# Layer 2 of the first chunk reordered: batch 1's transposes ahead of the second sub-block, squares of v and pieces of sums moved

## The chip, the cores and the metric

The kernel runs on one core of a Trainium2 chip. The metric is the device time of one execution in microseconds (us), lower is better. A core has five engines that this document names as the profile does: PE (TensorE, matrix products; PEld is its loading of weights, which overlaps), DVE (VectorE), ACT (ScalarE), POOL (GpSimd) and SP (SyncE). Each engine executes its own instructions strictly in the order in which the program issues them, and waits at an instruction whose inputs, or whose output's space, are not ready. Transfers from and to main memory (DMA) are issued here from the queues of SP and POOL and run beside the engines.

## The reference

Attention over 8 batches of 8 heads, 576 positions and head dimension 64, followed by a two-layer network on the 4608 tokens:

```python
scores = scale * (q @ k.transpose(0, 1, 3, 2))          # 8 x 8 x 576 x 576
cum = np.cumsum(np.maximum(s, 0.0), axis=-1)
bias = -(cum[:, :, :, None] - cum[:, :, None, :])
scores = np.where(causal, -1e9, scores + np.minimum(bias, 0.0))
attn = softmax(scores)
x = (attn @ v).transpose(0, 2, 1, 3).reshape(4608, 512)
h = x @ w_in                                            # 512 -> 2048
g = 0.5 * h * (1.0 + erf(h / sqrt(2)))                  # exact gelu
out = g @ w_out                                         # 2048 -> 512
```

## The kernel before, in words

**Tiling.** The tokens are worked through in nine chunks of 512. A chunk needs the attention of a batch (576 tokens), so the loop `for c in range(NCH)` does, for chunk c, layer 1 and then layer 2, and puts the attention of batch c + 1 between the matrix products of layer 2. Nothing is scheduled by a planner: the order of the calls in the program is the order on each engine. PSUM, where PE writes, is given out by name: three slots `x`, `y`, `z` of two banks each and two single banks `M[0]`, `M[1]`. A slot is free again when the engine that reads the last result in it has done so.

**Attention of a batch.** `tr_one` (or `tr_two`) transposes q or k of four heads on PE (L395: 36 small products) and copies the result from PSUM to `qkT` (L402 if ACT copies, L404 if DVE does). `sc_mm(b, p, slots)` computes the scores of a pair of heads in two units (10 products, L434), each followed by one exp on ACT into `P` (L440). `mask` multiplies the diagonal blocks of `P` on DVE (L448 twice and L453 once for a pair). `scale_v` multiplies tiles of v by decay weights on DVE (L247, five tiles). `av_main` multiplies `P` with the weights and with v on PE (L463), after which `av_out` computes a reciprocal on ACT as ln and exp (L478, L479) for two halves of 256 columns and multiplies on DVE into `xT` (L503). `av_tails` does the last 64 positions at the start of the next layer 1. `av_main(b, 0)` reads pairs 0 and 2 of `P`, `av_main(b, 1)` pairs 1 and 3.

**Layer 1 of chunk 0** is `l1_item(c, f2)` for f2 = 0 to 7: eight products of 512 columns into slot `order[c][f2 % 3]` (L550) and a gelu on ACT (L558, the last one in two halves, L561). Item 7 writes the slot that item 4's gelu has read. The DVE computes `absmax` of four pairs meanwhile (L229).

**Layer 2 of chunk 0** is `l2_item(c, sub, f0, f1)` for four sub-blocks of 128 tokens (L576). Each sub-block sums over 16 products; they are issued as 8, 4 and 4, because the weights `w_out_r` arrive in four transfers of four rows each (POOL queue, L270). Sub-blocks 0 and 1 stand in `M[0]` and `M[1]`, 2 and 3 in the two halves of slot `y`. The last four products of a sub-block are followed by a copy to `o_sb` (on ACT for sub-blocks 0, 1, 2, on DVE for 3) and a store on SP's queue (L779). Since `order[1] = (y, z, x)`, the first item of chunk 1's layer 1 needs slot `y`, so it waits for the copy of sub-block 3.

Between these stand the transposes of batch 1's q and k (`tr_one(1, qd, i, eng, slot)`: qd 0 serves pairs 0 and 1, qd 1 pairs 2 and 3), its four `sc_mm`, masks, `scale_v(1, STS)` and the two `av_main`. Further there are

- `squares_v(b)`: the sum of squares of v on ACT (L237, two activations and two reads of the accumulator), used only by a check at the kernel's end;
- `exp_set()`: loads ACT's function table for exp and ln (L863); gelu needs another table (loaded before L558). Squares run with either table;
- `sums_b(which, f0, f1)`: differences of blocks of `w_out_r` into four tiles `Ts` on DVE (L743), for indices f0 to f1 of 8; index f needs rows 2f and 2f + 1 of `w_out_r`. Chunk 1's layer 2 is the first to read them. The fourth sum reads the second;
- `behind(1, w_out_r[0:1, FT - 5, 0:D])` and `load_v(1)`: a tiny transfer on SP's queue that waits for row 11 of `w_out_r`, so that the five transfers of batch 1's v (L225) start after it;
- `behind_v(1, 1)`: a tiny copy on POOL that waits for tile 1 of that v, followed in POOL's queue by four `load_front(2, ...)` (L106) and by `load_qk(3, "q")` (L197).

The loads of batch 1's q and k, `load_front(1, ...)`, are issued by POOL during the start of layer 1 (L106), among the loads of `w_out_r`.

Of the kernel before, what the change touches and what calls it, by code (L numbers as in the profile page):

```python
# [19 lines left out]
def kernel(  # L20
# [10 lines left out]
    nc = tc.nc  # L31
# [66 lines left out]
    def bank(slot, shape, dtype, name):  # L98

        return ps.tile(shape, dtype, tag=slot, bufs=1, name=name)  # L100
# [141 lines left out]
    def scale_v(b, sts, eng, h0=0, h1=H):  # L242
        t = raws[b, "v"]
        vb = vv[b % 2]
        for st0, st1 in sts:
            n_st = 128 if st1 < ST else SL
            eng.tensor_tensor(  # L247
                vb[:n_st, st0:st1, h0:h1, :],
                t[:n_st, st0:st1, h0:h1, :],
                wb[:n_st, st0:st1, b * H + h0 : b * H + h1]  # L250
                .unsqueeze(3).to_broadcast([n_st, st1 - st0, h1 - h0, D]),
                op=MULT,
            )

    STS = [(st, st + 1) for st in range(ST)]
# [150 lines left out]
    def tr_two(b, qd, i, engs):  # L406
        t_ps = [bank(m, [128, FR, 64], bf16, "tr_ps") for m in M]
        tr_mm(b, qd, i, t_ps)
        for pp in range(2):
            copy(  # L410
                engs[pp],
                qkT[b % 2][:, i, 2 * qd + pp, :S].rearrange("d (t r) -> d t r", r=FR),
                t_ps[pp].rearrange("d r t -> d t r"),
            )
# [485 lines left out]
    for c in range(NCH):  # L900
        nb = c + 1
        if nb >= B:
            l1_seven(c)
            if c < B:
                order[c + 1] = order[c]
            sums_a(c, (1, 2), HF // 2, HF)
            l2_seven(c)
            continue
        if c < 2:
            l1_item(c, 0, 0, KO - 2)  # L910
            l1_item(c, 1, 0, KO - 2)
            av_tails(c, M[0])
            l1_item(c, 0, KO - 2)
            l1_item(c, 1, KO - 2)
        else:
            l1_item(c, 0, 0, KO - 2)
            l1_item(c, 0, KO - 2)
            l1_item(c, 1)
        if 1 < c:
            transpose_tiles(nb)  # L920
            if nb + 1 < B:
                behind_g(qkT[nb % 2][0:1, 1, NP - 1, S - 1 : S])
                for n in "qk":
                    load_qk(nb + 1, n)
        for p in range(NP) if c == 0 else (0, 1) if c == 1 else (0, 1, 2):
            absmax(c, p)
        for f2 in range(2, FT // 2):
            l1_item(c, f2)
            if c == 1 and 2 <= f2 < 6:
                tr_two(2, f2 // 2 - 1, f2 % 2, both)  # L930
            if c == 1 and f2 == 2:
                squares_v(1)
                load_qk(3, "k")
            if c == 1 and 3 <= f2 < 5:
                scale_v(2, STS[f2 - 3 : f2 - 2], nc.vector)
            if c == 1 and f2 == 5:
                sums_a(c, (1, 2, 3), 0, HF // 2)
                scale_v(2, STS[2:4], nc.vector)
                squares_v(2)
            if c > 1 and f2 == 3:  # L940
                scale_v(nb, [(0, 4), (4, 5)], nc.vector)
                sums_a(c, (1, 2, 3), 0, HF // 2)
                absmax(c, 3)
                if c == B - 2:
                    sums_u((1, 2))
                    absmax(nb, 0)
            if c > 1 and f2 == 4:
                squares_v(nb)
                if nb + 1 < B:
                    behind(2, raws[nb + 1, "k"][0:1, ST - 2, 0, :])  # L950
                    load_v(nb + 1, [nc.sync])
        if c == 0:
            squares_v(0)
            sums_b((1, 2, 3, 4), 0, 4)
            exp_set()
            x, y, z = order[0]
            l2_item(c, 0, 0, 8)
            l2_item(c, 1, 0, 8)
            tr_one(1, 0, 0, nc.vector, z)
            tr_one(1, 0, 1, nc.scalar, x)  # L960
            l2_item(c, 2, 0, 8, y)
            sc_mm(1, 0, (z, x))
            l2_item(c, 3, 0, 8, y)
            sc_mm(1, 1, (z, x))
            mask(1, 0, nc.vector)
            sums_b((1, 2, 3), 4, 8)
            behind(1, w_out_r[0:1, FT - 5, 0:D])
            load_v(1, [nc.sync])
            l2_item(c, 0, 8, 12)
            l2_item(c, 1, 8, 12)  # L970
            tr_one(1, 1, 0, nc.vector, z)
            tr_one(1, 1, 1, nc.scalar, x)
            mask(1, 1, nc.vector)
            sums_b((4,), 4, 8)
            behind_v(1, 1)
            for qd in range(2):
                for n in "qk":
                    load_front(2, n, qd)
            l2_item(c, 2, 8, 12)
            l2_item(c, 3, 8, 12)  # L980
            sc_mm(1, 2, (z, x))
            l2_item(c, 0, 12, eng=nc.scalar)
            sc_mm(1, 3, (z, x))
            mask(1, 2, nc.vector)
            scale_v(1, STS, nc.vector)
            l2_item(c, 1, 12, eng=nc.scalar)
            l2_item(c, 2, 12, eng=nc.scalar)
            mask(1, 3, nc.vector)
            av_main(1, 0, M[0], z)
            l2_item(c, 3, 12)  # L990
            av_main(1, 1, M[1], x)
            order[1] = (y, z, x)
            load_v(2, [nc.sync])
            load_qk(3, "q")
        else:
            exp_set()
            sums_a(c, (1, 2), HF // 2, HF)

            x, y, z = order[c]
            order[nb] = (z, x, y)  # L1000
            add = nc.vector.tensor_tensor
            al_t = bank(M[0], [128, 2, 256], fp32, "o_al")
            al = [al_t[:, u] for u in range(2)]
            kept = [keep_sb(i, n) for i, n in enumerate(("q0", "k0", "q1"))]
            oa = [two_sb() for _ in range(2)]

            prod(c, 1, al, start=True)
            sc_mm(nb, 0, (z, x))
            sc_mm(nb, 2, (y,))
            copy(nc.vector, kept[0], al_t)  # L1010
            if c == 1:
                scale_v(2, STS[4:5], nc.vector)
                load_v(3, [nc.sync])
            be = bank(M[1], [128, 2, 256], fp32, "o_be")
            prod(c, 2, [be[:, u] for u in range(2)], start=True)
            prod(c, 6, al, 0, 6)
            mask(nb, 0, nc.vector)
            add(oa[0][:, :, N1], be, kept[0], op=ALU.add)
            sc_mm(nb, 2, (z,), 1)
            sc_mm(nb, 1, (x, y))  # L1020
            mask(nb, 2, nc.vector)
            prod(c, 6, al, 6)
            copy(nc.vector, kept[1], al_t)
            mask(nb, 1, nc.vector)
            sc_mm(nb, 3, (z, x))
            sums_a(c, (3, 4), HF // 2, HF)
            sums_a(c, (4,), 0, HF // 2)
            ga_t = bank(M[1], [128, 2, 256], fp32, "o_ga")
            ga = [ga_t[:, u] for u in range(2)]
            prod(c, 5, ga, start=True)  # L1030
            mask(nb, 3, nc.vector)
            if nb + 1 < B:
                behind_g(P_of[nb, 3][0:1, 1, PW - 1 : PW])
                cast_qk(nb + 1)
            den = bank(z, [128, 2, 512], fp32, "av_d")
            o = av_pe(nb, 0, den[:, 0], y)
            av_out(nb, 0, den[:, 0], o)
            prod(c, 7, al)
            copy(nc.scalar, kept[2], al_t)
            o = av_pe(nb, 1, den[:, 1], x)  # L1040
            add(oa[1][:, :, N2], ga_t, kept[2], op=ALU.add)
            av_out(nb, 1, den[:, 1], o)
            prod(c, 4, al)
            if c == B - 2:
                sums_x(c + 1, nc.vector)
            av_tails(nb, y)
            copy(nc.scalar, oa[1][:, :, N1], al_t)
            if c == B - 2:
                nc.scalar.preload_act_table_set("gelu_and_others")
            store(c, 2, oa[1])  # L1050
            prod(c, 3, ga)
            add(oa[0][:, :, N2], ga_t, kept[1], op=ALU.add)
            store(c, 1, oa[0])
            if c == 1:
                absmax(1, 2)
                absmax(1, 3)
                square(7)
            elif nb < B - 1:
                square(c + 1 if c > 2 else 0)
            if c == 2:  # L1060
                cert_decay()
            if c == B - 2:
                sums_u((3,))
# [4 lines left out]
    with tc.If(rv > 0):  # L1068
        with tc.tile_pool(name="gen", bufs=1) as gen, tc.tile_pool(
# [26 lines left out]
            with tc.For_i(0, B, 1) as b:  # L1096
# [8 lines left out]
                for h in range(H):  # L1105
# [17 lines left out]
                    for it in range(ST):  # L1123
# [9 lines left out]
                        x = gen.tile([128, S], fp32, tag="gx", bufs=2, name="gx")  # L1133
# [88 lines left out]
```

## Time and profile before

| | |
|---|---|
| median of 3 runs | 314.04 us (313.4 to 314.63) |
| the profiled execution, its own time | 314.03 us |
| its span, first to last instruction | 312.2 us |
| granted TensorE clock | 0.994 |
| layer 1 of chunk 0 on PE | 22.4 to 36.8 us of the span |
| layer 2 of chunk 0 on PE | 36.8 to 59.4 us |
| layer 1 of chunk 1 on PE | from 59.4 us |

The profile is one execution; times in it count from the first instruction. A row of the timeline reads: start, busy time, engine, line, operation, output, inputs, shape, count, and in brackets how long the engine had stood idle and what ended that. A row of a busy PE does not say that products run at full rate; the end of a product overlaps the start of the next, so a step's length is taken from one start to the next start. In the view of groups a row ends with busy time, mean ns of one, and the idle time before them. A row of transfers ends with the time from issue to landing.

### The profile page before, as it was taken

How to read it: one execution, taken by the hardware profiler on the slowest of the kernel's cores; microseconds unless marked ns; L12 is line 12 of the kernel's file. 1: busy time of each engine (PE TensorE's matmuls, PEld its weight loads, DVE VectorE, ACT ScalarE, POOL GpSimd, SP SyncE). 2: the span in 40 equal slices, each digit the busy share in tenths (PEclk: the TensorE clock that was granted, in tenths of full speed). 3: DMA queues.
4: the chain of work that ended last, by engine and by line, in shares of the span. 5: the costliest groups of instructions: out<-in, count | busy, mean ns of one | idle time of the engine just before them, and what ended most of it. 6: DMA issues, size and time to landing. Idle time of an engine off the chain costs nothing.

```text
span 312.2 us, 8460 instructions
## 1 busy us (share of the span) xinstructions
PE 293.0 (94%) x3522; PEld 194.8 (62%) x3522; DVE 228.4 (73%) x430; ACT 246.7 (79%) x348; POOL 98.8 (32%) x180
## 2 busy tenths in 40 slices
PE   0689999999999999999999999999999999999991
PEld 0564444545784578547854786477647887887780
DVE  3597337788879777696876597748798889856770
ACT  3687687798968996989788988798879877967830
POOL 6585007104070376228530944095500000000000
PEclk9999999999999999999999999999999999999997
DMA  7999999996616696969597859967891030011013
GB/s 110 200 180 206 206 166 188 270 237 155 132 24 193 120 221 127 256 116 214 116 277 140 186 121 232 208 156 150 171 249 20 2 135 5 0 69 68 2 47 98
DMA packets 77933, 45.07 MB, mean 144 GB/s; under 512 B 63168, under 2 KB 70336, under 8 KB 77888
## 3 DMA queue, kind: packets, MB, share of 16 engines
q1 hardware_dynamic: 67104, 24.93, 35.0%
q0 software_dynamic: 10784, 19.53, 32.1%
q8 instruction: 29, 0.48, 0.7%
q14 instruction: 16, 0.13, 0.2%
HBM read 36.85 MB, written 9.44 MB: 148 GB/s over the span
## 4 chain that ended last, share of the span: by engine, by line
PE 84%; DVE 5%; ACT 5%; DMA 2%; issue 1%; POOL 0%; ACTq 0%; POOLq 0%
PE h_ps L550 32%; PE o_al L764 17%; PE o_ga L764 9%; PE h_ps L667 6%; PE sc_ps L434 5%; PE o_be L764 4%; PE av_o L463 4%; PE av_d L463 2%; DMA fk<-in_k_dram 2%; PE o_ps L576 2%; ACT junk L237 2%; ACT P L440 2%; DVE vv L247 2%; PE av_t L463 1%; PE tr_ps L395 1%
## 5 line engine op out<-in xcount | busy, mean ns | idle before, releaser
L550 PE MATMUL h_ps<-xT,w_in_r 128*128 128x512 f16 x480 | 106.4, 379 | 0.5 <-DVE o_sb L404 0.5
L550 PEld LDWEIGHTS <-w_in_r 128*128 128x128 f16 x480 | 46.3, 98 | 53.9 <-issue 0.8
L440 ACT ACTIVATE P<-sc_ps 128x1024 bf16<-128x1024 f32 x64 | 60.2, 1032 | 3.4 <-PE sc_ps L434 3.3
L558 ACT ACTIVATE gT<-h_ps 128x1024 f16<-128x1024 f32 x49 | 48.3, 1018 | 13.2 <-PE h_ps L550 13.0
L764 PEld LDWEIGHTS <-S 128*128 128x128 f16 x512 | 47.8, 98 | 8.4 <-issue 0.9
L229 DVE TENSOR_REDUCE amx<-qkT 128x2 f32<-128x1152 bf16 x32 | 41.6, 1345 | 0.3 <-DMA qkT<-qk_bf 0.3
L764 PEld LDWEIGHTS <-gT 128*128 128x128 f16 x384 | 36.5, 98 | 7.6 <-issue 2.2
L448 DVE TENSOR_TENSOR P<-P,tri_bf 128x512 bf16<-128x512 bf16 x64 | 25.9, 420 | 11.3 <-ACT P L440 10.7
L754 DVE TENSOR_TENSOR S<-gT 128x1024 f16<-128x1024 f16 (+1 forms) x30 | 21.6, 722 | 14.0 <-ACT gT L561 12.1
L764 PE MATMUL o_al<-T,S 128*128 128x256 f16 x256 | 31.7, 273 | 0.0
L197 POOL DMA_DIRECT2D raw_k<-in_k_dram x25 | 21.1, 850 | 13.8 <-DMA raw_v<-in_v_dram 13.8
L434 PE MATMUL sc_ps<-qkT 64*128 64x256 bf16 (+2 forms) x320 | 22.3, 264 | 3.0 <-DVE qkT L404 1.7
L503 DVE TENSOR_TENSOR xT<-av_o,ln 128x256 f16<-128x256 f32 (+2 forms) x72 | 23.8, 387 | 1.6 <-ACT ln L479 1.2
L247 DVE TENSOR_TENSOR vv<-raw_v,wb 128x512 bf16<-128x512 f32 (+2 forms) x25 | 24.0, 1002 | 0.0
L197 POOL DMA_DIRECT2D raw_q<-in_q_dram x25 | 21.1, 858 | 0.9 <-POOL seen_v L148 0.9
L434 PEld LDWEIGHTS <-qkT 64*128 64x128 bf16 x320 | 13.9, 98 | 12.0 <-issue 6.7
L237 ACT ACTIVATE junk<-raw_v 128x2048 bf16<-128x2048 f32 (+1 forms) x16 | 20.3, 1268 | 0.3
L404 DVE COPY qkT<-tr_ps 128x576 bf16<-128x576 bf16 (+1 forms) x15 | 12.0, 834 | 10.1 <-PE tr_ps L395 10.1
L681 DVE TENSOR_TENSOR k<-h_ps,k 128x512 f32<-128x512 f32 (+1 forms) x12 | 11.3, 956 | 8.1 <-PE h_ps L667 5.5
L479 ACT ACTIVATE ln<-ln,lnb 128x256 f32<-128x256 f32 x32 | 16.3, 509 | 1.0
L148 POOL CAST seen_v<-qkT 1x1 f32<-1x1 bf16 x4 | 1.2, 304 | 48.5 <-DMA qkT<-qk_bf 48.5
L463 PE MATMUL av_o<-P,vv 128*32 128x256 bf16 (+1 forms) x512 | 16.5, 270 | 0.0
(132 smaller groups left out, 439.2 us busy)
## 6 DMA issues: line engine op xcount, KB each, us to landing
raw_v<-in_v_dram SPq DMA_DIRECT2D x32, 256.0 KB, 4.8
out_dram<-o_sb SPq DMA_DIRECT2D x14, 512.0 KB, 4.0
raw_q<-in_q_dram POOLq DMA_DIRECT2D x20, 256.0 KB, 4.6
raw_k<-in_k_dram POOLq DMA_DIRECT2D x20, 256.0 KB, 6.6
w_out_r<-in_moe_w_out_dram POOLq DMA_DIRECT2D x4, 512.0 KB, 13.0
out_dram<-o_sb SPq DMA_DIRECT2D x7, 256.0 KB, 7.2
fq<-in_q_dram POOLq DMA_DIRECT2D x6, 288.0 KB, 7.0
fk<-in_k_dram POOLq DMA_DIRECT2D x6, 288.0 KB, 8.1
```

The source lines that it names most:

```text
L197: nc.gpsimd.dma_start(out=t[:n_st, st], in_=src)
L229: nc.vector.tensor_reduce(amx[:, b * NP + p], qkT[b % 2][:, :, p, :S], axis=AX, op=ALU.max, apply_absolute_value=True)
L237: nc.scalar.activation(n[:n_st, : (st1 - st0) * H * D], t[:n_st, st0:st1].rearrange("p s h d -> p (s h d)"), func=AF.Square, accum_out=amv ...
L247: eng.tensor_tensor(vb[:n_st, st0:st1, h0:h1, :], t[:n_st, st0:st1, h0:h1, :], wb[:n_st, st0:st1, b * H + h0 : b * H + h1] .unsqueeze(3).t ...
L434: nc.tensor.matmul(s_ps[:, e, off : off + n], lhsT=qkT[b % 2][e * 64 : e * 64 + 64, 1, p, jt * 128 : jt * 128 + 128], rhs=qkT[b % 2][e * 6 ...
L440: nc.scalar.activation(P[:, :, UO[u] : UO[u] + UW[u]], s_ps[:, :, : UW[u]], func=AF.Exp, scale=scale)
L448: eng.tensor_tensor(d, d, tri_bf.unsqueeze(1).unsqueeze(1).to_broadcast([128, 2, 2, 128]), op=MULT)
L463: nc.tensor.matmul(o[g * 32 : g * 32 + 32, lo : lo + n], lhsT=(wb[:, jt, b * H + 2 * g + qd : b * H + 2 * g + qd + 1].to_broadcast([128, 3 ...
L503: nc.vector.tensor_tensor(xT[:, 2 * qd + t, x0 : x0 + hi - lo], o[t][:, c * 256 + lo : c * 256 + hi], ln[:, c * 256 + lo : c * 256 + hi], ...
L550: nc.tensor.matmul(h_ps[:, i, :], lhsT=w_in_r[:, ko, ft * 128 : (ft + 1) * 128], rhs=xT[:, ko, c * NB % XW : c * NB % XW + NB], start=(ko ...
L558: nc.scalar.activation(gT_of[c][:, f2 * 2 : f2 * 2 + 2, :], h_ps, func=AF.Gelu)
L764: nc.tensor.matmul(o[u], lhsT=lhs[:, f, u * 128 : u * 128 + 128], rhs=rhs[:, f], start=start and j == 0 and (by_sub or u == 0), stop=j == ...
```

## The change

In layer 1 of chunk 0, after item 3, come `squares_v(0)` (which stood at the start of layer 2, after item 7's gelus) and the first half of the sums over `w_out_r`. In layer 2 the transposes of qd 0 come after eight products instead of sixteen; the two `sc_mm` of pairs 0 and 1 come one sub-block earlier each; the transposes of qd 1 come ahead of the second round of sub-blocks 0 and 1 instead of behind it; `sc_mm` of pairs 2 and 3 come earlier too, and the last four products of sub-blocks 0, 1 and 2 stand together. The sums are cut into smaller pieces, and the last piece of the fourth goes to layer 1 of chunk 1. `scale_v(1)` is cut in two, with the mask of pair 2 between.

```diff
@@ layer 1, for f2 in range(2, FT // 2), after l1_item(c, f2)
+            if c == 0 and f2 == 3:
+                squares_v(0)
+                sums_b((1, 2, 3, 4), 0, 2)
...
             if c == 1 and f2 == 5:
                 sums_a(c, (1, 2, 3), 0, HF // 2)
                 scale_v(2, STS[2:4], nc.vector)
+                sums_b((4,), 4, 8)
                 squares_v(2)
@@ layer 2
         if c == 0:
-            squares_v(0)
-            sums_b((1, 2, 3, 4), 0, 4)
+            sums_b((1, 2, 3, 4), 2, 4)
             exp_set()
             x, y, z = order[0]
             l2_item(c, 0, 0, 8)
-            l2_item(c, 1, 0, 8)
             tr_one(1, 0, 0, nc.vector, z)
             tr_one(1, 0, 1, nc.scalar, x)
+            l2_item(c, 1, 0, 8)
+            sc_mm(1, 0, (z, x))
             l2_item(c, 2, 0, 8, y)
-            sc_mm(1, 0, (z, x))
+            mask(1, 0, nc.vector)
+            sc_mm(1, 1, (z, x))
             l2_item(c, 3, 0, 8, y)
-            sc_mm(1, 1, (z, x))
-            mask(1, 0, nc.vector)
-            sums_b((1, 2, 3), 4, 8)
+            sums_b((1, 2, 3), 4, 6)
             behind(1, w_out_r[0:1, FT - 5, 0:D])
             load_v(1, [nc.sync])
+            tr_one(1, 1, 0, nc.vector, z)
+            tr_one(1, 1, 1, nc.scalar, x)
             l2_item(c, 0, 8, 12)
             l2_item(c, 1, 8, 12)
-            tr_one(1, 1, 0, nc.vector, z)
-            tr_one(1, 1, 1, nc.scalar, x)
             mask(1, 1, nc.vector)
-            sums_b((4,), 4, 8)
             behind_v(1, 1)
             for qd in range(2):
                 for n in "qk":
                     load_front(2, n, qd)
+            sc_mm(1, 2, (z, x))
+            sums_b((1, 2, 3), 6, 8)
+            scale_v(1, STS[0:2], nc.vector)
             l2_item(c, 2, 8, 12)
             l2_item(c, 3, 8, 12)
-            sc_mm(1, 2, (z, x))
-            l2_item(c, 0, 12, eng=nc.scalar)
+            mask(1, 2, nc.vector)
             sc_mm(1, 3, (z, x))
-            mask(1, 2, nc.vector)
-            scale_v(1, STS, nc.vector)
-            l2_item(c, 1, 12, eng=nc.scalar)
-            l2_item(c, 2, 12, eng=nc.scalar)
+            scale_v(1, STS[2:5], nc.vector)
+            for i in range(3):
+                l2_item(c, i, 12, eng=nc.scalar)
             mask(1, 3, nc.vector)
             av_main(1, 0, M[0], z)
             l2_item(c, 3, 12)
```

## The prediction, written before the changed kernel was run

> **What bounds the kernel now.** First the page's busy times, then the stretch that the diff touches.
>
> ```profile
> span 312.2 us, 8460 instructions
> PE 293.0 (94%) x3522; PEld 194.8 (62%) x3522; DVE 228.4 (73%) x430; ACT 246.7 (79%) x348; POOL 98.8 (32%) x180
> 36.60:59.40 22.80, 21.58 (x347) 10.97 (x345) 14.04 (x30) 19.05 (x27) 7.23 (x10) 1.00 1.08 191
> ```
>
> The third row is from the view by stretches: length, then PE, PEld, DVE, ACT and POOL busy. PE fills 94% of the kernel and 21.58 of the 22.80 us of layer 2 of chunk 0, at full clock (1.00). So this change can give little more than PE's standstill there. The timeline of PE shows where it stands:
>
> ```profile
> 36.83 3.62 PE L576 MATMUL o_ps<-w_out_r,gT 128*128 128x512 f16 x16
> 40.37 0.48 PE L395 MATMUL tr_ps<-ident_bf,fq 64*64 64x64 bf16 x36
> 41.11 1.90 PE L576 MATMUL o_ps<-w_out_r,gT 128*128 128x512 f16 x8
> 43.24 0.61 PE L434 MATMUL sc_ps<-qkT 64*128 64x256 bf16 x10 [0.23 <-ACT qkT L402]
> 43.78 1.90 PE L576 MATMUL o_ps<-w_out_r,gT 128*128 128x512 f16 x8
> ...
> 52.16 0.39 PE L434 MATMUL sc_ps<-qkT 64*128 64x256 bf16 x4
> 53.07 0.40 PE L434 MATMUL sc_ps<-qkT 64*128 64x256 bf16 x6 [0.52 <-ACT P L440]
> 53.40 1.90 PE L576 MATMUL o_ps<-w_out_r,gT 128*128 128x512 f16 x8
> 55.23 0.57 PE L463 MATMUL av_d<-P,wb 128*32 128x256 bf16 x16
> ...
> 56.63 1.04 PE L576 MATMUL o_ps<-w_out_r,gT 128*128 128x512 f16 x4
> 57.60 0.57 PE L463 MATMUL av_d<-P,wb 128*32 128x256 bf16 x16
> ...
> 59.40 1.89 PE L550 MATMUL h_ps<-xT,w_in_r 128*128 128x512 f16 x8 [0.47 <-DVE o_sb L404]
> ...
> 88.97 0.57 PE L463 MATMUL av_d<-P,wb 128*32 128x256 bf16 x16
> ...
> 90.24 1.92 PE L764 MATMUL o_al<-T,gT 128*128 128x256 f16 x16
> ```
>
> Step lengths, start to start: eight products 1.83 us (53.40 to 55.23), a pair's scores 0.54 (43.24 to 43.78), both transposes 0.74 (40.37 to 41.11), four products 0.97 (56.63 to 57.60), an `av_main` 1.27 (88.97 to 90.24, in chunk 1). By these the standstills are 0.30 us before 43.24 (41.11 + 1.83 = 42.94), 0.70 around 53.07 (the pair's scores took from 52.16 to 53.40, 1.24 for 0.54), 0.13 in the first `av_main` (55.23 to 56.63, 1.40) and 0.53 at the end (57.60 + 1.27 = 58.87). What PE waits for is read from the chain that ended last:
>
> ```profile
> 38.11 1.90 ACT junk L237 x2
> ...
> 40.77 0.49 ACT L863
> ...
> 42.06 1.13 ACT qkT L402
> ...
> 53.61 3.00 DVE vv L247 x5
> ...
> 57.42 1.33 DVE xT L503 x4
> 58.75 0.61 DVE o_sb L404
> ```
>
> Early, ACT holds it: squares, table load, copy of k. Late, DVE: five tiles of v, a mask, products into xT, and the copy that frees slot y. In all 0.30 + 0.70 + 0.13 + 0.53 = **1.66 us** is PE's standstill, the ceiling of the gain.
>
> **The change part by part.** *Squares in layer 1.*
>
> ```profile
> 31.84 1.02 ACT L558 ACTIVATE gT<-h_ps 128x1024 f16<-128x1024 f32 x1 [0.70 <-PE h_ps L550]
> ...
> 37.02 1.08 ACT L561 ACTIVATE gT<-h_ps 128x512 f16<-128x512 f32 x2 [0.70 <-PE h_ps L550]
> ...
> 66.60 1.92 ACT L237 ACTIVATE junk<-raw_v 128x2048 bf16<-128x2048 f32 x1
> ...
> 69.28 1.91 ACT L558 ACTIVATE gT<-h_ps 128x1024 f16<-128x1024 f32 x2
> ```
>
> Item 3's gelu ends 0.70 before 31.84, at 31.14. In chunk 1 the same squares hold ACT from 66.60 to 69.28, 2.68 us. So item 4's gelu moves from 31.84 to about 33.75 and ends at 34.77. Item 7 writes item 4's slot; PE reaches it at 35.10 (36.83 less eight products at 1.73), 0.33 later. Item 5's gelu then ends near 35.7, item 6's near 36.65, and the last starts at 37.02 as before. Cost nothing, covered by ACT's 0.70 us per item; if the 0.33 were gone, each further us is PE's.
>
> *First transposes.* PE does eight products (36.83 to 38.65), transposes until 39.40 and has the second sub-block until 41.23. The last gelu ends at 38.10, the table load then takes 1.29 (40.77 to 42.06), and the copy of k 1.13: ready at 40.5. DVE's copy of q is ready at the same time (its 1.36 us from 39.18). The 0.30 us standstill goes, with 0.7 to spare. That these transposes read loads which are not moved is a rival below.
>
> The Trainium skill ("ScalarE: Activation LUTs", What ACT_TABLE_LOAD costs) states about 2.66 us for a switch of table, a load of 1283 ns and a drain of 1380 ns. By that the copy of k would end at 41.9 and PE would stand 0.65 us. The row disagrees, the next instruction starts 1.29 us after the load.
>
> *Scores.* One exp takes 1.03 us, two at most 2.06; PE needs 0.54 + 1.83 = 2.37 between two score pairs:
>
> ```profile
> L440 ACT ACTIVATE P<-sc_ps 128x1024 bf16<-128x1024 f32 x8 | 7.8, 1029 | 1.9 <-PE sc_ps L434 1.9
> L448 DVE TENSOR_TENSOR P<-P,tri_bf 128x512 bf16<-128x512 bf16 x8 | 3.2, 420 | 4.2 <-ACT P L440 4.2
> L743 DVE TENSOR_TENSOR T<-w_out_r 128x1024 f16<-128x1024 f16 x2 | 1.4, 684 | 0.0
> ```
>
> So pairs at 41.2, 43.6, 48.6 and 50.9 find their slots free; before, pairs 2 and 3 had only four products between them (0.97), which made the 0.70 standstill. It goes: eight products stand there now. The second transposes (from 46.0) need the exps of pair 1, done at about 46.0.
>
> *DVE.* In layer 1 it waits for `w_out_r` with nothing else to do:
>
> ```profile
> 34.24 0.69 DVE L743 TENSOR_TENSOR T<-w_out_r 128x1024 f16<-128x1024 f16 x1 [3.16 <-DMA w_out_r<-in_moe_w_out_dram]
> ```
>
> Wherever the first sums stand, they are done by 37, long before DVE's copy at 39.2; they cost nothing. The cut sums are of 512 elements, which the trace has as no sum; the nearest row is the mask's, 420 ns at 512, against 684 at 1024. Ends 342 and 684; I take 420, since type and size match. DVE's order from 46.5: copy of q 1.36, mask 0.85, three sums 1.2, two tiles of v 1.2 (five in 3.00, above), mask 0.85 (exp done 50.9), three tiles 1.8, mask 0.85: done at 54.7. PE reaches `av_main` at 54.2 and needs v, done at 53.8, about 0.4 later, and pair 3 at 56.4: no wait, the 0.13 goes. At 684 a sum DVE is 0.8 later, which is just in time for v; at 342, 0.2 earlier, nothing changes. The fourth sum's last piece, 0.69 us, falls into chunk 1 ahead of this:
>
> ```profile
> 77.66 0.69 DVE L754 TENSOR_TENSOR S<-gT 128x1024 f16<-128x1024 f16 x1 [0.59 <-ACT gT L561]
> ```
>
> Of it 0.59 lies in DVE's idle time, 0.1 is left, and DVE waits for exps 0.3 us soon after. Cost nothing; without that cover 0.7 on DVE.
>
> *The end.* All of PE's work to the end of the second `av_main` is the same, so it ends at 58.87 − 0.30 − 0.70 − 0.13 = 57.74, with the first starting at 54.2 (57.74 less two of 1.27 and 0.97). Slot y is late next:
>
> ```profile
> 55.19 1.12 ACT L402 COPY o_sb<-o_ps 128x512 f32<-128x512 f32 x2
> 56.13 0.46 ACT L478 ACTIVATE ln<-av_d 128x256 f32<-128x256 f32 x1
> ...
> 57.44 0.51 ACT L479 ACTIVATE ln<-ln,lnb 128x256 f32<-128x256 f32 x1
> ```
>
> ACT has exps of pair 3 until 53.4, then three copies at 0.56, the last not before 54.3 because its products end at 54.2: until 55.0. ln starts there; from 56.13 to 57.95 are 1.82, so the second reciprocal is ready at 56.85. DVE's products with it take 0.7 (half of 1.33), the copy of sub-block 3 0.65: 58.2, and layer 1 starts at **58.3 instead of 59.4**. PE stands some 0.55 there, as before: the 0.30, 0.70 and 0.13 are won, 1.13 us; ends for it are 0.9 (with the long sums DVE's products into xT start late) and 1.66.
>
> *Queues.*
>
> ```profile
> 43.04 5.12 SPq L225 DMA_DIRECT2D raw_v<-in_v_dram  x5
> raw_v<-in_v_dram SPq DMA_DIRECT2D x1, 128.0 KB, 4.6
> 49.02 0.70 POOL L106 DMA_DIRECT2D fq<-in_q_dram  x1 [0.34 <-PE tr_ps L395]
> ```
>
> No transfer changes its place in SP's or POOL's queue. The loads of v start at 43.04 by their own gate, and the last (issue about 47.2 to 48.2) lands by 52.8; DVE wants that tile at about 53.2. The mask of pair 2 and all behind it now stand behind tiles 0 and 1; these have landed by 48.7, where POOL goes on (49.02 less 0.34), and DVE wants them at 49.9. POOL no longer waits 0.34 for transposes, so batch 2's fronts start that much earlier. Stores of sub-blocks 0 to 2 go out up to 0.6 us later, which nothing waits for, and batch 2's v, behind the store of sub-block 3, 1 us earlier with everything else. Later stages follow PE, so the shift stays.
>
> **Sum.** The profiled execution took 314.03 us, 312.2 of span and 1.83 around it. Less 1.13: **312.9 us**, as against the median too (314.04), −0.36%. About 0.5% (1.57 us) is what a measurement of this kernel can tell from no change; its three runs spread over 1.2 us.
>
> **Rivals.**
> - *All standstill goes* (1.66 us, 312.4). For it: the squares give ACT 2.7 us, and slot y is freed by a copy that only its queue makes late. Against it: ACT's copies and reciprocals ahead are tied to the products just before them. It needs the end 0.55 us shorter than the rows. 17%.
> - *The table switch takes longer here*, right behind the gelus, than behind the squares: at twice its row (2.58) the copy of k ends at 41.8 and PE stands 0.55 at the first scores, 313.5. The 1.29 between load and next instruction speaks against. 5%. This is the mechanism of the section cited above.
> - *Little is won*: gelu 4 late by over 0.33 us, the long sums, or a later stage whose transfers don't move up; 0.4 or less is left, 314.0. 10%.
> - *Slower: q and k of batch 1 land behind the transposes.* PE now reaches k at 38.95, and in PE's order everything stands behind it.
>
> ```profile
> 23.82 0.71 POOL L106 DMA_DIRECT2D fk<-in_k_dram  x1
> fk<-in_k_dram POOLq DMA_DIRECT2D x1, 288.0 KB, 13.2
> ```
>
> It landed at 37.0 (37.7 if counted from the issue's end), among 13 us of other transfers. Each us past 38.95 costs one; past 40.1 the gain is gone, past 41.6 it is over 0.5% slower: some 316. Against it: a slip of over 4 us is a third of the landing time. 10%.
>
> **How the numbers follow.** Forecast 58%, with 312.5 to 313.3 its own range before the runs' spread of some 0.6 either way. The range 312.1 to 314.4 takes in the forecast with that spread, the drain, little won and most of the full win; left out are the slower case and the edges. Faster by over 0.5% (below 312.5): a fifth of the forecast, 12%, and most of the full win, 12%: 24%. Slower by over 0.5%: nearly all of the last case, 9%. Within: 67%.
>
> **What would show it.** Layer 2 starts at 36.8; the first pair's scores at 41.2 without a wait; no wait of PE for an exp of pair 3; `av_main` at 54.2; first product of chunk 1 at 58.3, waiting some 0.5 us for DVE's copy of `o_sb`. It is wrong if PE waits for `fk` or at item 7 for a gelu, if `av_o` waits for v, or if the start of chunk 1 moves but the end doesn't.

## The result, and the profile after

| | before | changed |
|---|---|---|
| median of 6 runs each | 314.09 us (313.4 to 314.85) | 312.26 us (311.55 to 312.99) |
| ratio, 95% interval | | 0.9938 (0.9915 to 0.9961) |
| the profiled execution, its span | 314.03 us, 312.2 us | 311.55 us, 309.8 us |
| layer 1 of chunk 0, first product | 22.41 us | 21.80 us |
| layer 2 of chunk 0, first product | 36.83 us | 36.22 us |
| layer 1 of chunk 1, first product | 59.40 us | 57.34 us |
| **stretch**: layer 2 of chunk 0 to layer 1 of chunk 1 | 22.57 us | 21.12 us |
| from there to the end of the span | 252.8 us | 252.46 us |

The change makes the kernel faster by 0.6% (0.4 to 0.85%). The two spans differ by 2.4 us, of which the stretch that the diff rewrites has 1.45. The other 0.61 lie ahead of layer 1, where both programs are the same, and 0.34 behind the start of chunk 1; the experiments say what these are.

The view by stretches of the changed kernel, from the first product of layer 2 to the first of chunk 1 (length, then PE, PEld, DVE, ACT and POOL busy):

```profile
36.22:57.34 21.12, 20.89 (x346) 10.86 (x344) 13.42 (x30) 16.36 (x23) 7.22 (x10) 1.00 1.11 194
```

PE's idle time has shrunk from 1.2 us to 0.23, and ACT has 2.7 us less to do in the stretch. PE's busy time has shrunk too, from 21.35 us (36.83 to 59.40 of the kernel before) to 20.89: part of a standstill lies in rows that count as busy, as around pair 3's scores before, where 0.52 of the 0.70 stood in brackets. The timeline of PE:

```profile
36.22 1.89 PE L576 MATMUL o_ps<-w_out_r,gT 128*128 128x512 f16 x8
...
38.34 0.50 PE L395 MATMUL tr_ps<-ident_bf,fk 64*64 64x64 bf16 x36
38.77 1.90 PE L576 MATMUL o_ps<-w_out_r,gT 128*128 128x512 f16 x8
40.60 0.61 PE L434 MATMUL sc_ps<-qkT 64*128 64x256 bf16 x10
...
50.30 0.61 PE L434 MATMUL sc_ps<-qkT 64*128 64x256 bf16 x10
50.85 2.76 PE L576 MATMUL o_ps<-w_out_r,gT 128*128 128x512 f16 x12
53.55 0.57 PE L463 MATMUL av_d<-P,wb 128*32 128x256 bf16 x16
...
54.81 1.04 PE L576 MATMUL o_ps<-w_out_r,gT 128*128 128x512 f16 x4
55.78 0.57 PE L463 MATMUL av_d<-P,wb 128*32 128x256 bf16 x16
...
57.34 1.89 PE L550 MATMUL h_ps<-xT,w_in_r 128*128 128x512 f16 x8 [0.23 <-DVE o_sb L404]
```

The bracketed waits for the copy of k and for an exp of pair 3 are gone, and so is the standstill at v (the first `av_main` takes 1.26 us, 53.55 to 54.81); one wait is left, for the copy that frees slot y. The squares in layer 1, in the timeline of ACT:

```profile
30.43 1.90 ACT L237 ACTIVATE junk<-raw_v 128x2048 bf16<-128x2048 f32 x1
...
33.08 2.81 ACT L558 ACTIVATE gT<-h_ps 128x1024 f16<-128x1024 f32 x3
36.42 1.09 ACT L561 ACTIVATE gT<-h_ps 128x512 f16<-128x512 f32 x2 [0.52 <-PE h_ps L550]
37.52 1.28 ACT L863 ACT_TABLE_LOAD   x1
38.90 1.12 ACT L402 COPY qkT<-tr_ps 128x1152 bf16<-128x1152 bf16 x1
```

Three gelus run back to back behind the squares, ACT has caught up by 36.42 (it waits for PE again), and layer 1 takes PE 14.42 us in both kernels (22.41 to 36.83, 21.80 to 36.22). The table load starts 1.30 us behind layer 2's first product instead of 3.94, and the copy of k ends at 40.02, ahead of the scores at 40.60.

### The profile page after: what moved, and what is told of

Read it like the earlier page. It is cut to its first block, busy times and chain, and to the rows that moved or that the text cites. A ratio compares the mean times of both kernels' runs of the same rounds, so it can differ in the third digit from the quotient of the medians.

```text
span 309.8 us, 8465 instructions
## 1 busy us (share of the span) xinstructions
PE 292.9 (95%) x3522; PEld 195.1 (63%) x3522; DVE 229.0 (74%) x437; ACT 246.4 (80%) x348; POOL 98.5 (32%) x180
## 4 chain that ended last, share of the span: by engine, by line
PE 88%; DVE 3%; ACT 3%; DMA 2%; issue 1%; POOL 0%; ACTq 0%; POOLq 0%
PE h_ps L550 33%; PE o_al L764 17%; PE o_ga L764 10%; PE h_ps L667 6%; PE sc_ps L434 5%; PE o_ps L576 4%; PE o_be L764 4%; PE av_o L463 4%; PE av_d L463 3%; DMA fk<-in_k_dram 2%; PE tr_ps L395 1%; PE av_t L463 1%; DVE qkT L404 1%; ACT P L440 1%; ACT junk L237 1%
```

## The experiments

All experiments compute the whole reference. The times of the kernel before, taken beside them, are medians of 313.86 to 313.93 us. The stretch is read from the timeline of PE.

### The same two kernels again: what is chance

No edit: `a1_before_again` is the kernel before, `a2_after_again` and `a3_after_third` are the changed one.

> The kernel before, unchanged, timed against itself: ratio 1.000, and its spread says what chance gives. Theory: the changed kernel's profile differs from the one of before by 0.61 us ahead of layer 1 and by 0.35 us at the end, where the programs are the same; if that is chance, this profile's first product of layer 1 of chunk 0 lies anywhere from 21.5 to 22.6 us, while its stretch from the first product of layer 2 of chunk 0 to the first product of chunk 1 is 22.57 again within 0.1. Rival: the start and the stretch are tied, and then the stretch moves with the start.

> The changed kernel again. Theory: the stretch of layer 2 of chunk 0 is 21.12 us again within 0.1, which is 1.45 less than before, and the median lies 1.2 to 1.9 us below before's. Rival (a good part of the 1.83 us between the medians is chance): under 1.2 us.

> The changed kernel a third time, on the same chip as the next one. Theory: stretch 21.12, median 1.3 to 1.8 us below before.

Measured: before again 313.83 us, ratio 1.0001 (0.9986 to 1.0015); changed again 312.38 us, 0.9954 (0.9938 to 0.9971), and 312.03 us, 0.9946 (0.9927 to 0.9964). From the timeline of PE of the kernel before, again:

```profile
21.79 1.90 PE L550 MATMUL h_ps<-xT,w_in_r 128*128 128x512 f16 x8
...
36.21 3.62 PE L576 MATMUL o_ps<-w_out_r,gT 128*128 128x512 f16 x16
...
58.79 1.89 PE L550 MATMUL h_ps<-xT,w_in_r 128*128 128x512 f16 x8 [0.47 <-DVE o_sb L404]
```

Its stretch is 22.58 us, against 22.57, although it starts 0.62 us earlier than the first profile of the same program. The changed kernel's is 21.12 in all three profiles. So the 1.45 us belong to the change, and the 0.61 at the start are chance: the kernel before has them too. So is the end: from the first product of chunk 1 to the end of the span it takes 252.8 and 253.11 us in two executions of before. The three comparisons of the changed kernel, 0.9938, 0.9954 and 0.9946, all hold 0.9954, which is 1.45 us of 314.

### Each part of the early chain alone

`e1_squares_only`, on the kernel before:

```diff
             l1_item(c, f2)
+            if c == 0 and f2 == 3:
+                squares_v(0)
...
         if c == 0:
-            squares_v(0)
```

> The kernel before with only the squares of batch 0's v moved into layer 1. Theory (the squares only open the way for earlier scores): the 0.30 us standstill ahead of the first scores goes, the 0.70 at pair 3, the 0.13 at v and the 0.53 at the end stay: stretch 22.27, some 0.3 us less than before. Rival (ACT is what bounds the stretch, and 2.7 us less on it is worth most of the gain): stretch under 21.6.

Measured: 313.38 us, ratio 0.9990 (0.9966 to 1.0014). The timeline of PE:

```profile
36.22 3.62 PE L576 MATMUL o_ps<-w_out_r,gT 128*128 128x512 f16 x16
...
42.34 0.61 PE L434 MATMUL sc_ps<-qkT 64*128 64x256 bf16 x10
...
52.08 0.40 PE L434 MATMUL sc_ps<-qkT 64*128 64x256 bf16 x6 [0.52 <-ACT P L440]
...
58.41 1.89 PE L550 MATMUL h_ps<-xT,w_in_r 128*128 128x512 f16 x8 [0.47 <-DVE o_sb L404]
```

The stretch is 22.19, 0.38 less than before, and the waits for the exp of pair 3 (0.52) and for slot y (0.47) are the same to the hundredth. The first scores no longer wait: they start 6.12 us behind the first product instead of 6.41. That is 0.29, what the expectation had. The rest lies in the second transposes, which take 0.74 us here (47.09 to 47.83) and 0.82 before; they come up again below. So the 2.7 us taken from ACT are worth 0.3 by themselves.

`e2_squares_back`, on the changed kernel:

```diff
             if c == 0 and f2 == 3:
-                squares_v(0)
                 sums_b((1, 2, 3, 4), 0, 2)
...
         if c == 0:
+            squares_v(0)
             sums_b((1, 2, 3, 4), 2, 4)
```

> The changed kernel with the squares back at the head of layer 2, all else as changed. Theory: the copy of k is ready at 42.6 instead of 40.0 (squares 2.77 ahead of it), the first scores stand about 2.0 us, and nothing takes that back: stretch 23.15, slower than before by some 0.6 us. Rival (the order of the later steps carries the gain, and the early wait is made up behind): stretch under 22.

Measured: 314.56 us, ratio 1.0024 (1.0001 to 1.0047), just slower than before. The timeline of PE:

```profile
36.13 1.89 PE L576 MATMUL o_ps<-w_out_r,gT 128*128 128x512 f16 x8
...
42.55 0.61 PE L434 MATMUL sc_ps<-qkT 64*128 64x256 bf16 x10 [1.96 <-ACT qkT L402]
...
59.28 1.89 PE L550 MATMUL h_ps<-xT,w_in_r 128*128 128x512 f16 x8 [0.23 <-DVE o_sb L404]
```

The stretch is 23.15, as expected, 2.03 above the changed kernel's. The new order needs the squares out of the way; without that it costs 0.58 us. Together with the run before: neither part is the gain, the two together are.

### Eight products between the scores of pairs 2 and 3, in the old order

`e3_eight_between`, on the kernel before:

```diff
             l2_item(c, 0, 12, eng=nc.scalar)
+            l2_item(c, 1, 12, eng=nc.scalar)
             sc_mm(1, 3, (z, x))
             mask(1, 2, nc.vector)
             scale_v(1, STS, nc.vector)
-            l2_item(c, 1, 12, eng=nc.scalar)
             l2_item(c, 2, 12, eng=nc.scalar)
```

> The kernel before with one line moved: sub-block 1's last four products stand ahead of pair 3's scores, so that eight products instead of four lie between the scores of pairs 2 and 3. The prediction's step (four products were what made the 0.70 us standstill) taken alone gives 0.7 less: stretch 21.9. Theory now: pair 3's exps then stand behind two copies on ACT and end near 56.0, so ln starts at 56.5 instead of 56.1, and DVE's five tiles of v and pair 3's mask end where they did; the standstill comes back in the end: stretch 22.6 to 22.9, none won.

Measured: 314.31 us, ratio 1.0008 (0.9992 to 1.0023). Rows of the timeline of PE, and then of the other engines:

```profile
37.67 3.62 PE L576 MATMUL o_ps<-w_out_r,gT 128*128 128x512 f16 x16
...
48.84 0.48 PE L395 MATMUL tr_ps<-ident_bf,fq 64*64 64x64 bf16 x36
...
49.58 1.90 PE L576 MATMUL o_ps<-w_out_r,gT 128*128 128x512 f16 x8
...
53.79 0.61 PE L434 MATMUL sc_ps<-qkT 64*128 64x256 bf16 x10
...
55.30 0.57 PE L463 MATMUL av_d<-P,wb 128*32 128x256 bf16 x16
...
56.84 0.62 PE L463 MATMUL av_o<-P,vv 128*32 128x128 bf16 x20 [0.31 <-DVE vv L247]
57.40 1.04 PE L576 MATMUL o_ps<-w_out_r,gT 128*128 128x512 f16 x4
...
60.16 1.89 PE L550 MATMUL h_ps<-xT,w_in_r 128*128 128x512 f16 x8 [0.47 <-DVE o_sb L404]
```

```profile
53.81 0.43 DVE L448 TENSOR_TENSOR P<-P,tri_bf 128x512 bf16<-128x512 bf16 x1 [0.49 <-ACT P L440]
...
54.29 3.08 DVE L247 TENSOR_TENSOR vv<-raw_v,wb 128x512 bf16<-128x512 f32 x5
...
58.11 1.40 DVE L503 TENSOR_TENSOR xT<-av_o,ln 128x256 f16<-128x256 f32 x4
...
59.44 0.68 DVE L404 COPY o_sb<-o_ps 128x512 f32<-128x512 f32 x1
```

The wait for the exp is gone, and yet the stretch is 22.49, only 0.08 less than before. Even these 0.08 stand ahead of the line that was moved: the second transposes take 0.74 us (48.84 to 49.58) instead of 0.82. The edit itself won nothing. The first `av_main` now takes 2.10 us (55.30 to 57.40) where it needs 1.27: PE stands 0.83 at the tiles of v instead of 0.13, the 0.70 moved there whole, and as long as ever at slot y. DVE goes without a break from pair 2's exp (53.81) to the copy of sub-block 3: mask, five tiles, mask, products, copy. With DVE's work in this order the chain begins when pair 2's scores are done, so it takes earlier scores of pair 2 to end it earlier. Whether the tiles of v ahead of pair 2's mask, in the old order on PE, would do it too, no run tries. The expectation had the outcome, none won, but put it on ACT and 0.1 to 0.4 us too late.

### DVE's pieces

`e5_dve_as_before`, on the changed kernel, puts the sums and the tiles of v back into the pieces and places of before, and leaves the squares and PE's order as changed:

```diff
-                sums_b((1, 2, 3, 4), 0, 2)
...
-                sums_b((4,), 4, 8)
...
-            sums_b((1, 2, 3, 4), 2, 4)
+            sums_b((1, 2, 3, 4), 0, 4)
...
-            sums_b((1, 2, 3), 4, 6)
+            sums_b((1, 2, 3), 4, 8)
...
-            sums_b((1, 2, 3), 6, 8)
-            scale_v(1, STS[0:2], nc.vector)
+            sums_b((4,), 4, 8)
...
-            scale_v(1, STS[2:5], nc.vector)
+            scale_v(1, STS, nc.vector)
```

> The changed kernel with DVE's work in the pieces and places of before: sums whole, five tiles of v together behind pair 2's mask. Theory (squares and the order on PE carry all; sums and pieces of v are free): stretch 21.12 within 0.1. Rival (DVE held the late part of the old chain, so its pieces are what brought it in time): 21.4 to 21.8, with PE waiting for v or for a mask.

Measured: 312.49 us, ratio 0.9963 (0.9945 to 0.9982). The timeline of PE:

```profile
36.90 1.89 PE L576 MATMUL o_ps<-w_out_r,gT 128*128 128x512 f16 x8
...
58.02 1.89 PE L550 MATMUL h_ps<-xT,w_in_r 128*128 128x512 f16 x8 [0.23 <-DVE o_sb L404]
```

21.12 to the hundredth, with no wait for v or a mask. In the new order DVE is early enough in either form: the lines of the diff that cut and move the sums and the tiles of v change nothing in the stretch.

### The wait that is left

`e6_copy_on_act` and `e6b_copy_on_act_again`, on the changed kernel:

```diff
             av_main(1, 0, M[0], z)
-            l2_item(c, 3, 12)
+            l2_item(c, 3, 12, eng=nc.scalar)
```

> The changed kernel with sub-block 3's copy on ACT instead of DVE. Theory (the 0.29 us left at the end is DVE's order, products into xT ahead of the copy; ACT is idle for 0.50 us just then): PE goes on without a wait, stretch 20.85, 0.27 less than the changed kernel and 1.7 less than before. Rival (xT for the first four heads would be what PE waits for next, or ACT's second ln is pushed back and the next stage pays): stretch 21.0 or more, or the gain gone by the first product of layer 2 of chunk 1.

> The changed kernel with sub-block 3's copy on ACT, again, beside the changed kernel on the same chip. Theory: stretch 20.83, and a median 0.29 below the changed kernel's, which the spread of the runs may hide. Rival (the earlier result, 2.0 us below before, showed more than the stretch): a median over 0.6 us below the changed kernel's.

Measured: 311.72 us, ratio 0.9935 (0.9918 to 0.9953), and 311.97 us, 0.9939 (0.9923 to 0.9955). Rows of the timeline, of the first:

```profile
36.75 1.89 PE L576 MATMUL o_ps<-w_out_r,gT 128*128 128x512 f16 x8
...
56.42 0.58 ACT L402 COPY o_sb<-o_ps 128x512 f32<-128x512 f32 x1
...
57.58 1.90 PE L550 MATMUL h_ps<-xT,w_in_r 128*128 128x512 f16 x8
```

The copy falls into ACT's gap between the two reciprocals, PE goes on without a wait, and the stretch is 20.83 in both profiles, 0.29 less than the changed kernel's and 1.74 less than before's. By its stretch this is the best of the versions here. On one chip the medians were 311.97 against the changed kernel's 312.03: the runs of the two spread over 1.55 and 3.18 us, so their times don't show 0.29. Besides, both profiled executions lost more than that ahead of the stretch, where the programs are the same: layer 1 of chunk 0 took 15.05 and 15.09 us instead of 14.42, with PE waiting for `w_in_r` (0.47 and 0.51). No profile of the changed kernel has that wait; whether it is chance, two executions don't tell.

### Loads of q and k that come later

`e7_fronts_swapped` and `e7b_fronts_swapped_again`, and `e8_fronts_last`, on the changed kernel:

```diff
e7
-    for qd in range(2):
+    for qd in (1, 0):
         for n in "qk":
             load_front(1, n, qd)
e8
+    for i in range(2, 4):
+        load_w_out(i)
     for qd in range(2):
         for n in "qk":
             load_front(1, n, qd)
-    for i in range(2, 4):
-        load_w_out(i)
```

> The changed kernel with batch 1's loads of q and k in the other order, so that the first transposes read the third and fourth of them; k is then issued at about 26.1 and, at 12.8 us, lands near 38.9, where PE wants it at 38.3 and wanted it at 40.7 in the old order. Theory (each us past PE's arrival costs one): PE waits some 0.5 us for k and the stretch is 21.6 (21.1 to 22.4). Rival (the wait is made up at the end, where PE stands 0.29 anyway): 21.3 or less with a wait for k shown.

> The kernel with batch 1's loads of q and k in the other order, again. Its profiled execution waited 0.34 us for k, its median was a further 0.7 us higher than that gives. Theory (when k lands moves by a us from one execution to the next, and in this order each us counts): another wait for k in this profile, between 0.2 and 1.5 us, and a stretch of 21.12 plus that wait. Rival (something else in these executions costs time): the same 0.34 and still the higher median.

> The changed kernel with batch 1's loads of q and k issued behind the last two transfers of w_out. Theory (the early transposes live on the loads landing in time; past PE's arrival at about 38.4 each us costs one): k lands near 41, PE stands some 2.7 us at the transposes, stretch 23.8 (23.0 to 25.5), slower than before by 0.5 to 2.5 us. Rival (the loads land in time anyway, since the queue isn't full): stretch 21.1.

Measured: swapped 313.38 us, ratio 0.9990 (0.9976 to 1.0003), and 313.43 us, 0.9993 (0.9971 to 1.0014); last 316.72 us, 1.0093 (1.0062 to 1.0124). The timeline of PE, of the first and second execution of the swapped order and of the last:

```profile
36.74 1.89 PE L576 MATMUL o_ps<-w_out_r,gT 128*128 128x512 f16 x8
...
39.22 0.48 PE L395 MATMUL tr_ps<-ident_bf,fk 64*64 64x64 bf16 x36 [0.18 <-DMA fk<-in_k_dram]
...
58.20 1.89 PE L550 MATMUL h_ps<-xT,w_in_r 128*128 128x512 f16 x8 [0.23 <-DVE o_sb L404]
```

```profile
36.27 1.89 PE L576 MATMUL o_ps<-w_out_r,gT 128*128 128x512 f16 x8
38.52 0.48 PE L395 MATMUL tr_ps<-ident_bf,fq 64*64 64x64 bf16 x36 [0.35 <-DMA fq<-in_q_dram]
39.94 0.48 PE L395 MATMUL tr_ps<-ident_bf,fk 64*64 64x64 bf16 x36 [0.95 <-DMA fk<-in_k_dram]
...
58.92 1.89 PE L550 MATMUL h_ps<-xT,w_in_r 128*128 128x512 f16 x8 [0.23 <-DVE o_sb L404]
```

```profile
36.94 1.89 PE L576 MATMUL o_ps<-w_out_r,gT 128*128 128x512 f16 x8
39.90 0.48 PE L395 MATMUL tr_ps<-ident_bf,fq 64*64 64x64 bf16 x36 [1.06 <-DMA fq<-in_q_dram]
41.56 0.48 PE L395 MATMUL tr_ps<-ident_bf,fk 64*64 64x64 bf16 x36 [1.19 <-DMA fk<-in_k_dram]
...
60.53 1.89 PE L550 MATMUL h_ps<-xT,w_in_r 128*128 128x512 f16 x8 [0.23 <-DVE o_sb L404]
```

The stretches are 21.46, 22.65 and 23.59. What is above 21.12 (0.34, 1.53 and 2.47) is the time that PE stood for q and k, to 0.03: without the waits k's transposes start 2.12 us behind the first product (36.22 to 38.34), here 2.48, 3.67 and 4.62, or 0.36, 1.55 and 2.50 later. So lateness is paid in full, and the wait at the end (0.23 in all three) gives none of it back. Two executions of one program differ by 1.2 us in this order, and by none where the loads have time to spare. For the last kernel the profiled execution, 315.03 us, was the shortest of four; that the others waited longer for the same loads is likely but not shown.

## Why the prediction came out as it did

The forecast was 312.9 us, in a range of 312.1 to 314.4, with 67% for a change of at most 0.5%. The median of 312.26 lies in the range; the ratio of 0.9938 lies beyond 0.5%, in the case that was given 24%, with an interval that holds both. What the change does to its stretch, 1.45 us or 0.46%, lies on the near side: it gives 312.6 from 314.04, inside the forecast's own range. The medians differ by 1.83 us here and by 1.55 and 1.83 when repeated; what is beyond 1.45 lies outside the stretch, where the profiles differ by chance, so it is luck of the executions, not the change's doing, that the ratio fell beyond 0.5%, as far as they show. The mechanism was right, and one term was mis-sized. By its steps:

- **Squares in layer 1: right.** Item 4's gelu was put at 33.75 on the clock of before (its rows add up to 33.82), or 33.14 with the start 0.61 earlier; it came at 33.08, and PE did not wait.
- **First transposes: right.** First scores at 41.2 on the clock of before; they came at 40.60, 0.61 earlier like all else, without a wait. The table switch behind the gelus (load at 37.52) held up nothing: the copy of k starts at 38.90, right behind its transposes (38.34 and 0.50). The rival built on a longer switch is out.
- **Pair 3's 0.70 us: right, with half a reason.** "Eight products stand there now" is not enough: alone it won nothing (the run with eight between). It goes because all scores come earlier, pair 2's too, which is where DVE's late chain begins: from them to `av_main` PE has 5.62 us of work now (47.93 to 53.55), where it had 4.58 with the standstill in it (50.65 to 55.23).
- **Sums and pieces of v at nothing: right.** A sum of 512 elements took 0.42 us, the value taken; with the old pieces the stretch is the same 21.12.
- **The end: the step that failed, in size.** "PE stands some 0.55 there, as before": it stood 0.29 (57.34 less 55.78 and 1.27). The chain of what ended last in the changed kernel shows why:

```profile
53.62 0.53 PE av_d L463 x16
...
54.16 0.39 ACT ln L478
...
55.39 0.52 ACT ln L479
...
55.93 0.76 DVE xT L503 x2
56.69 0.61 DVE o_sb L404
...
57.34 1.89 PE h_ps L550 x8
```

  From the start of `av_main` (53.55) to the end of the copy (57.30) it is 3.75 us; the prediction had 4.0. ln started 0.61 behind `av_main`, not 0.8. The prediction had it wait for the three copies on ACT; these began at 52.62 (53.4 less 0.61 is 52.8) and took 1.61 together, not 3 x 0.56, so they were done within 0.1 us of the end of the products into `av_d` (54.14), and by the chain it is these products that released ln. The second reciprocal, which waits for nothing else, starts 0.62 behind its `av_main` (55.78 to 56.40). The reciprocals took 1.75 and not 1.82, whose first ln took 0.46, against 0.39; the copy took 0.61, not 0.65. Only the products into xT took longer (0.78 to the copy, not 0.7). Small terms, nearly all to one side, on the step that sets the end.
- **Not counted:** the second transposes took 0.82 us in before (47.99 to 48.81), 0.83 in its repetition, and 0.73 or 0.74 in the other kernels' profiles. That is 0.08, and with the 0.24 at the end it makes up the 0.32 between 1.13 and 1.45. It went with the squares alone too, and with an edit that stands behind the transposes, so it is no part of the mechanism forecast. Its cause no row names.
- **Later stages follow PE: right.** From the first product of chunk 1 to the first product of the last chunk's layer 2 both kernels take 232.9 us (59.40 to 292.31, 57.34 to 290.27), and from there on too they keep step: from the first product of chunk 1 to the last group of products it is 244.10 to 244.14 us in all fourteen profiles of this document.
- **The slower rival: the mechanism is real, and it was not near.** In the changed kernel k was issued at 22.95 and landed 13.1 later, at 36.05, 2.3 us ahead of PE. With the loads two places later most of the gain is gone by the medians, and behind two more transfers of `w_out` the kernel is 0.9% slower than before.
- **All standstill goes (17%):** not by this change, but by one more word in it, the copy on ACT. What spoke against it in the prediction, ACT's work tied to the products just ahead, was right for the changed order; what it overlooked is ACT's gap of 0.50 us between the two reciprocals.

## What to carry to other kernels

When one engine is busy almost throughout, count its standstill in the stretch from start-to-start differences: that is about the ceiling of a reordering there, and here the changed order with one more edit reached it (1.66 counted, 1.74 won with the 0.08 of the second transposes). A wait that is removed alone may only move to the next link; look for where that link's chain begins, and move the whole chain ahead. Before moving work earlier, compare its arrival with the landing of the loads that it reads: here loads that landed 2.3 us ahead cost nothing, and what they came late was paid in full, and differently in each execution.

## What the runs showed of the hardware that was not expected

A stretch in which nothing waits for a transfer repeats to the hundredth of a microsecond: 21.12 in three profiles of the changed kernel and one with other DVE work, 20.83 twice, 22.57 and 22.58 for before. The spread that the profiles show, of times that vary by some 2 us in the kernel before, lies where transfers set the pace. The first product of layer 1, ahead of which PE waits 5.9 to 6.8 us for q and 0.7 to 1.6 for k, came between 21.66 and 22.71 us in the profiles here. Layer 1 of chunk 0 took 14.41 or 14.42 us in nine of them and 14.52 to 15.09 in five, of which two have the wait for `w_in_r`. At the end, from DVE's last copy of a result, with its store behind it, to the end of the span, it took 7.05 us in one execution of before (304.85 to 311.9) and 5.95 in that of the kernel with the squares back (305.35 to 311.3), where the programs are the same. For a change of less than 2 us the timeline of its stretch says more than the medians.
